# Half-height projection tiles, a parameter chain on GpSimd and an earlier set of rotation matrices in an attention-plus-SSM kernel

## The chip, the cores and the metric

The kernel runs on one core of one Trainium2 chip. The core has a matrix engine (TensorE, PE in the profile, with its weight loads as PEld), three engines for elementwise work (VectorE or DVE, ScalarE or ACT, GpSimd or POOL) and a synchronising engine (SyncE, SP), which here only issues transfers; ACT issues a few too. Each engine works through its own queue in order and waits on semaphores. The metric is device time in microseconds (us), lower is better; the profile's span is a little shorter than the time of the same execution.

## The reference

Two independent branches of 2048 tokens and 448 channels; their outputs stand side by side.

```python
# A: attention, 16 heads of 28, each token looks at 8 earlier tokens, 2 apart
qkv = x @ wqkv
logits = einsum("bhsd,bhswd->bhsw", q, kg) * scale      # kg: k at s, s-2, ..., s-14
attn = softmax(where(mask, logits, -1e9))
a = einsum("bhsw,bhswd->bhsd", attn, vg) -> [S, 448] @ wo
# B: a diagonal complex state-space layer with 448 states
Lam_bar = exp(exp(log_dt) * Lam)
B_bar = ((Lam_bar - 1) / Lam)[:, None] * Bmat
Bu = einsum("bld,pd->blp", x, B_bar)
h_t = Lam_bar * h_{t-1} + Bu_t
b = 2 * real(h @ Cmat^T) + x * Dskip
out = concatenate([a, b], -1)                            # bfloat16
```

## The kernel before

**Branch A.** Token p*16+j sits in partition p (0 to 127) with j = 0 to 15, so the eight keys of a token are in its own partition or, for the first few j, in a halo of 14 that transfers copy from the partition below. The x of branch A is transposed on PE, two j at a time (`g_xta`, group jp holds j = 2jp and 2jp+1; eight groups, taken from jp = 7 down), in four blocks of 112 channels, and DVE copies the result from PSUM to `xTA`. A projection (`proj(t, j)`, t = 0 for q, 1 for k, 2 for v) is then four matmuls of 112 contraction rows by 448 columns into one PSUM bank, which ACT copies out (L326) into `q_s`, `k_s` or `v_s`. There are 48 projections. `logits(hf, n, g)` puts DVE work on a list: for a half of the j (`hf`) and two offsets, one large product of q and k (L500) and a tree of additions (L503 to L517); eight of them. Softmax follows on DVE and ACT, then 40 products of weights and v (L573), which PE transposes and sums (L592) and multiplies by wo (L609).

**Branch B.** The states lie in seven groups of 64, real and imaginary parts in the two halves of the 128 partitions. Time is cut in pieces of T = 8 steps. Seven rotation matrices `R[k]` (one for each power of the state transition, built by DVE from small coefficients, L207), a pair `G` for B_bar (built the same way), and cosine and sine tables `tab` for the long scan all come from the parameters. These start as 28 short rows (`prow`, four small loads on ACT's queue), are transposed on PE (`params_in`), and go through a chain of about 35 tiny operations on [128, 7] and [128, 56] tiles: `params1` (to phases and exponents), `params_act` (exp and sines on ACT), `params2` (the rotation coefficients), `params3` (the coefficients of G). All of it but `params_act` is on DVE. `tables` (L299 to L302) computes the phases of the scan tables on DVE in three large operations, with R[1] to R[4] as scratch; six ACT operations turn them into `tab` (the list `acts`). `build_D` makes a diagonal matrix of Dskip on DVE, for the skip term.

PE work of branch B: `b_weights` (B times G), `b_x` (transposes of branch B's x, copied by ACT), `c_weights`, `ssm_in` (input sums and the 8 steps within a piece, first for four state groups, then for three), the scan over pieces (`scan_mul` and `scan_run` on DVE, `scan_pe` on PE), `ssm_mix` (adds the carried state to each step), `ssm_out` (eleven matmuls into one bank: C, then the skip diagonal; ACT copies it out).

**Order.** The schedule is written by hand. PE, ACT and SP get their instructions in program order; DVE work is put on a list with a cost (`add`) and taken off it when a running count of DVE time falls behind a running count of PE time (`pe`, `pump`, `fit`), or when `need` asks for it. The PSUM has eight banks, taken in turn by `bank()`: whoever asks for a bank waits until the tile that had it eight requests earlier has been read. Transfers take one of eight landing semaphores in turn; the ninth waits at its queue for the first to have landed. Before, ACT's queue starts with the four parameter rows, and SP's with x of branch A in five pieces of whole rows (tokens 14 and 15 first), the three thirds of wqkv, then B, branch B's x (rows cut in 384 and 64 columns) and C.

The main sequence is: groups 7 and 6, then k of j = 15 to 6 with the parameter chain between, q of j = 15 to 8 (after which the first logits can start), k of j = 5 to 0, all v with `b_weights`, q of j = 7 to 0 with `b_x`, then branch B's sums and scan, its outputs, and branch A's second half.

Of the kernel before, what the change touches and what calls it, by code (L numbers as in the profile page):

```python
# [14 lines left out]
J = 16  # L15
HALO = 14
# [20 lines left out]
def kernel(  # L37
# [48 lines left out]
    xnA = u1.rearrange("p (j d) -> p j d", j=J)  # L86
# [4 lines left out]
    wts = wbuf[0:KT].rearrange("p (a k n) -> p a k n", a=3, k=4)  # L91
# [3 lines left out]
    xTA = u3[0:KT].rearrange("p (k j n) -> p k j n", k=4, j=J)  # L95
# [3 lines left out]
    w_r = A_wqkv.rearrange("(k p) n -> p k n", p=KT)  # L99
    xB_r = B_x[0].rearrange("(c p j) d -> p c j d", p=128, j=T)  # L100

    def load_w(t):
        SP.dma_start(wts[:, t], w_r[:, :, t * D:(t + 1) * D])

    def load_x(lo, hi):
        SP.dma_start(xnA[:, lo:hi, :], xA_r[:, lo:hi, :])
# [5 lines left out]
    for i, vec in enumerate((B_Lambda_re, B_Lambda_im, B_log_dt, B_Dskip)):  # L112
        ACT.dma_start(prow[NT * i:NT * (i + 1)], vec.rearrange("(t i) -> t i", i=HS).unsqueeze(1).to_broadcast((NT, 2, HS)))
# [4 lines left out]
    load_x(4, 8)  # L118
    load_w(0)
    load_x(0, 4)  # L120
    load_w(2)
    SP.dma_start(Bn[0:HS, :, 0:D], half_rows(B_B_re))
# [73 lines left out]
    def tt(o, a_, b_, op):  # L196
        V.tensor_tensor(o, a_, b_, op)
        return o
# [23 lines left out]
    def params_in():  # L222
        tp = bank(BF16)
        PE.transpose(tp[:, 0:4 * NT], prow.rearrange("p a i -> p (a i)"), ident[0:4 * NT, 0:4 * NT])
        V.tensor_copy(prm.rearrange("p a b -> p (a b)"), tp[:, 0:4 * NT])
        ACT.activation(dt[:], ld, ACTF.Exp)
        dve(0.3)

    def params1():
        tt(are[:], dt[:], lre, ALU.mult)  # L230
        tt(th[:], dt[:], lim, ALU.mult)
        tt(rk[:], by_k(are), kkb, ALU.mult)
        V.tensor_scalar(f1[:], th[:], 1.0 / (2 * PI), None, ALU.mult)
        V.tensor_scalar(fT[:], th[:], float(T) / (2 * PI), None, ALU.mult)
        tt(yk[:], by_k(f1), kkb, ALU.mult)
        V.tensor_scalar(tk[:], yk[:], 1.0, MAGIC, ALU.mult, ALU.add)
        V.scalar_tensor_tensor(tk[:], tk[:], -MAGIC, yk[:], ALU.add, ALU.subtract)
        tt(den[:], lre, lre, ALU.mult)
        tt(t0[:], lim, lim, ALU.mult)
        tt(den[:], den[:], t0[:], ALU.add)  # L240
        V.reciprocal(den[:], den[:])
        dve(1.7)
# [7 lines left out]
    def params2():  # L250
        def two(ap):
            return ap.unsqueeze(3).to_broadcast((HS, T - 1, NT, 2))
        tt(sn[:], sn[:], rk[:], ALU.mult)
        V.tensor_copy(coef[0:HS, :, :, 1], two(sn[0:HS, 0:T - 1]))
        V.tensor_scalar(coef[HS:128, :, :, 0], two(sn[HS:128, 0:T - 1]), -1.0, None, ALU.mult)
        tt(cs[:], cs[:], rk[:], ALU.mult)
        V.tensor_copy(coef[0:HS, :, :, 0], two(cs[0:HS, 0:T - 1]))
        V.tensor_copy(coef[HS:128, :, :, 1], two(cs[HS:128, 0:T - 1]))

    def params3():  # L260
        a1, b1 = cs[:, 0], sn[:, 0]
        V.tensor_scalar(nr[:], a1, -1.0, None, ALU.add)
        tt(gre[:], nr[:], lre, ALU.mult)
        tt(t0[:], b1, lim, ALU.mult)
        tt(gre[:], gre[:], t0[:], ALU.add)
        tt(gre[:], gre[:], den[:], ALU.mult)
        tt(gim[:], b1, lre, ALU.mult)
        tt(t0[:], nr[:], lim, ALU.mult)
        tt(gim[:], gim[:], t0[:], ALU.subtract)
        tt(gim[:], gim[:], den[:], ALU.mult)  # L270
        V.tensor_copy(cg[0:HS, :, 0], gre[0:HS])
        V.tensor_copy(cg[0:HS, :, 1], gim[0:HS])
        V.tensor_scalar(cg[HS:128, :, 0], gim[HS:128], -1.0, None, ALU.mult)
        V.tensor_copy(cg[HS:128, :, 1], gre[HS:128])
        cg2 = cg.unsqueeze(3).to_broadcast((128, NT, 2, 2))
        V.tensor_copy(cgb[:, 0], cg2)
        tt(cgb[:, 1], cg2, cgb[:, 0], ALU.subtract)
# [10 lines left out]
    def build_D():  # L288
        V.tensor_copy(dsk[0:HS], prm[0:HS, 3, 0:NT:2])
        V.tensor_copy(dsk[HS:128, 0:3], prm[HS:128, 3, 1:NT:2])  # L290
        V.tensor_copy(dsk[HS:128, 3:4], prm[HS:128, 3, NT - 1:NT])
        V.tensor_tensor(dgD.rearrange("p (k n) -> p k n", k=4), ident.unsqueeze(1).to_broadcast((128, 4, 128)),
                        dsk.unsqueeze(2).to_broadcast((128, 4, 128)), ALU.mult)

    yy = tab.rearrange("p a t c -> p (a t c)").bitcast(F32).rearrange("p (t c) -> p t c", t=NT)
    tm = R[:, 1:5].rearrange("p k t n -> p (k t n)").bitcast(F32).rearrange("p (t c) -> p t c", t=NT)

    def tables():
        V.tensor_tensor(yy, iot.unsqueeze(1).to_broadcast((128, NT, NC)),  # L299
                        fT.unsqueeze(2).to_broadcast((128, NT, NC)), ALU.mult)  # L300
        V.tensor_scalar(tm, yy, 1.0, MAGIC, ALU.mult, ALU.add)
        V.scalar_tensor_tensor(tm, tm, -MAGIC, yy, ALU.add, ALU.subtract)  # L302
        for t in (slice(0, 4), slice(4, NT)):
            acts.append(lambda t=t: ACT.activation(tab[:, 1, t], tm[:, t], ACTF.Sin, scale=-2 * PI * SHR))
            acts.append(lambda t=t: ACT.activation(tm[:, t], tm[:, t], ACTF.Abs))
            acts.append(lambda t=t: ACT.activation(tab[:, 0, t], tm[:, t], ACTF.Sin, bias=hpib[:], scale=-2 * PI * SHR))


    def g_xta(jp):
        tp = bank(BF16)  # L310
        tpv = tp[0:KT].rearrange("p (k j n) -> p k j n", k=4, j=2)
        for kt in range(4):
            for jj in range(2):
                PE.transpose(tpv[:, kt, jj, :], xnA[:, 2 * jp + jj, KT * kt:KT * (kt + 1)], ident[:])  # L314
        V.tensor_copy(xTA[:, :, 2 * jp:2 * jp + 2, :], tpv)  # L315
        dve(0.65)
        load[0] += 0.45

    def proj(t, j):
        ps = bank()  # L320
        for kt in range(4):
            PE.matmul(ps[:, 0:D], xTA[:, kt, j, :], wts[:, t, kt, :], start=(kt == 0), stop=(kt == 3))  # L322
        src = ps[:, 0:D].rearrange("p (h d) -> p d h", h=H)
        dst = (q_s[:, :, j * H:(j + 1) * H] if t == 0 else
               k_s[:, :, HALO + j, :] if t == 1 else v_s[:, HALO + j])
        ACT.copy(dst, src)  # L326
        count[2] += 1
        if acts and count[2] > 18 and count[2] % 2 == 0:
            acts.pop(0)()
        pe(0.76)  # L330
# [137 lines left out]
    def ssm_out(j, cb):  # L468
        cols = slice(cb * 128, (cb + 1) * 128)
        ps = bank()  # L470
        for t in range(NT):
# [5 lines left out]
        PE.matmul(ps[:, 384:448], xT[:, jp, 6, cols], dgD[:, 384 + HS * jj:384 + HS * (jj + 1)], start=False, stop=True)  # L477
# [3 lines left out]
        pe(1.53)  # L481
# [3 lines left out]
    Ls = [Lf[:, 0:1024].rearrange("p (w n) -> p w n", w=W), Lf[:, 1024:2048].rearrange("p (w n) -> p w n", w=W)]  # L485
    m4 = Lf[:, 2048:2560].rearrange("p (w n) -> p w n", w=4)
    attn = u3[:, 5120:7168].rearrange("p (w n) -> p w n", w=W)
# [135 lines left out]

    g_xta(7)
    g_xta(6)
    proj(1, 15)
    proj(1, 14)
    params_in()
    g_xta(5)
    params1()  # L630
    proj(1, 13)
    proj(1, 12)
    params_act()
    g_xta(4)
    proj(1, 11)
    proj(1, 10)
    g_xta(3)
    add(1.2, params2)
    has_R = [add(0.6, lambda: build_R(0))]
    add(2.3, params3)  # L640
    has_G = add(1.1, build_G)
    proj(1, 9)
    proj(1, 8)
    g_xta(2)
    proj(1, 7)
    proj(1, 6)
    has_tab = add(5.2, tables)
    has_D = add(1.1, build_D)
    has_B2 = add(0.3, double_B)
    proj(0, 15)  # L650
    g_xta(1)
    proj(0, 14)
    g_xta(0)
    for j in range(13, 7, -1):
        proj(0, j)
    logits(1, 0, 3)
    for j in range(5, -1, -1):
        proj(1, j)
# [5 lines left out]
    for j in range(15, -1, -1):  # L664
        proj(2, j)
        if j % 2 == 0 and j > 0:
            b_weights(j // 2 - 1)
        elif j in (7, 3):
            b_x(0, j // 4)
    for k in range(1, T - 1):  # L670
        has_R.append(add(0.55, lambda k=k: build_R(k)))
    halo(lambda lo, hi, a_, b_: v_s[lo:hi, a_:b_])
    for j in range(7, -1, -1):
        proj(0, j)
        if j % 2 == 1:
            b_x(2 - j // 4, j // 2 % 2)
    for n_, g in enumerate((0, 1, 2, 3)):
        logits(0, n_, g)
# [8 lines left out]
    for n_ in range(8):  # L687
        next(first)
        if n_ in (1, 2):
            b_x(3, n_ - 1)  # L690
# [3 lines left out]
    need(has_tab)  # L694
    while acts:
        acts.pop(0)()
# [23 lines left out]
    ssm_mix(0, 2)  # L720
    banks = scan_pe(1, 1)
# [3 lines left out]
    need(has_D, *has_R)  # L725
    ssm_mix(0, 3)
    ssm_mix(0, 4)
    ssm_mix(0, 5)
    banks = scan_pe(1, 0)
# [11 lines left out]
    for cb in range(2):  # L741
        ssm_out(T - 1, cb)
    for j in range(T - 1):
        if j + 1 < T - 1:
            ssm_mix(1, j + 1)
        for cb in range(2):
            ssm_out(j, cb)
# [42 lines left out]
```

## Time and profile before

| | us |
|---|---|
| median of 3 runs (lowest, highest) | 166.61 (166.44, 167.23) |
| the profiled execution, its time | 167.04 |
| the profiled execution, its span | 165.2 |
| PE busy, DVE busy, ACT busy, POOL busy | 157.0, 146.2, 101.2, 2.9 |
| granted PE clock | full in all 40 slices |
| first transposes of x (PE) | 4.82 |
| second group of transposes, after a wait for its x | 6.56 |
| first product of the logits (DVE, L500) | 27.32 |
| first scan product (DVE, L427) | 74.73 |
| first product of weights and v (DVE, L573) | 119.62 |

Busy time on PE is the union of pipelined matmuls and does not say that each ran at its best rate; the pitch of matmuls in a row does. "[0.94 <-DVE wbuf L427]" behind a row of the timeline is idle time of that engine before the row, and what ended it. "x12" is a number of merged instructions. In the chain of waits a row is a start, a length and what held the end of the kernel in that time.

### The profile page before, as it was taken

How to read it: one execution, taken by the hardware profiler on the slowest of the kernel's cores; microseconds unless marked ns; L12 is line 12 of the kernel's file. 1: busy time of each engine (PE TensorE's matmuls, PEld its weight loads, DVE VectorE, ACT ScalarE, POOL GpSimd, SP SyncE). 2: the span in 40 equal slices, each digit the busy share in tenths (PEclk: the TensorE clock that was granted, in tenths of full speed). 3: DMA queues.
4: the chain of work that ended last, by engine and by line, in shares of the span. 5: the costliest groups of instructions: out<-in, count | busy, mean ns of one | idle time of the engine just before them, and what ended most of it. 6: DMA issues, size and time to landing. Idle time of an engine off the chain costs nothing.

```text
span 165.2 us, 3640 instructions
## 1 busy us (share of the span) xinstructions
PE 157.0 (95%) x1511; PEld 110.9 (67%) x1513; DVE 146.2 (89%) x178; ACT 101.2 (61%) x194; POOL 2.9 (2%) x23
## 2 busy tenths in 40 slices
PE   6799999999999999997997999999999999999992
PEld 6566655666667878774764666665659988877870
DVE  1377999999999999998999999999999999999911
ACT  3068568999997474693569865579431343436531
POOL 3000000000000000000010000000000000000000
PEclk9999999999999999999999999999999999999999
DMA  5999996796299000000000002111214001112112
GB/s 157 341 250 186 237 269 137 147 158 90 50 194 145 4 4 0 0 4 0 0 4 0 0 5 81 57 56 63 76 62 125 31 28 60 57 43 74 64 51 83
DMA packets 17164, 14.01 MB, mean 85 GB/s; under 512 B 6636, under 2 KB 16636, under 8 KB 17020
## 3 DMA queue, kind: packets, MB, share of 16 engines
q1 hardware_dynamic: 17063, 13.77, 35.5%
q8 instruction: 12, 0.20, 0.5%
q14 instruction: 5, 0.04, 0.1%
q10 hardware_dynamic: 84, 0.01, 0.0%
HBM read 6.89 MB, written 3.67 MB: 64 GB/s over the span
## 4 chain that ended last, share of the span: by engine, by line
PE 56%; DVE 33%; issue 6%; DMA 3%; SPq 0%; DVEq 0%
PE b L322 22%; DVE k_s L573 11%; PE b L472 7%; PE b L592 6%; DVE u L500 5%; PE b L609 5%; PE b L382 3%; DMA u<-in_A_x_dram 3%; DVE u L503 2%; PE b L314 2%; PE b L462 2%; PE b L460 2%; DVE k_s L577 2%; DVE R L207 2%; PE b L337 2%
## 5 line engine op out<-in xcount | busy, mean ns | idle before, releaser
L322 PE MATMUL b<-wbuf,u 112*128 112x448 bf16 x192 | 39.6, 352 | 0.0
L573 DVE TENSOR_TENSOR k_s<-u,v_s 128x1792 bf16<-128x1792 bf16 (+1 forms) x40 | 33.1, 897 | 0.0
L500 DVE TENSOR_TENSOR u<-q_s,k_s 128x7168 bf16<-128x7168 bf16 x8 | 31.1, 3887 | 0.2
L592 PEld LDWEIGHTS <-k_s 128*112 128x112 bf16 x448 | 26.9, 130 | 2.5 <-DVE k_s L577 0.7
L592 PE MATMUL b<-ident,k_s 128*112 128x128 bf16 x448 | 27.4, 219 | 0.3 <-DVE k_s L577 0.3
L322 PEld LDWEIGHTS <-u 112*128 112x128 bf16 x192 | 17.9, 98 | 14.0
L472 PE MATMUL b<-Cw,u 128*128 128x448 bf16 x112 | 23.8, 352 | 0.0
L402 ACT CAST u<-b 128x512 bf16<-128x512 f32 (+1 forms) x32 | 15.6, 542 | 11.2 <-PE b L401 8.8
L382 PE MATMUL b<-xT,BT 128*128 128x256 bf16 x168 | 20.7, 273 | 0.0
L382 PEld LDWEIGHTS <-BT 128*128 128x128 bf16 x168 | 16.2, 98 | 2.4 <-issue 0.2
L503 DVE TENSOR_TENSOR u<-u 128x3584 bf16<-128x3584 bf16 x8 | 16.2, 2023 | 0.2
L614 ACT CAST ya<-b 128x448 bf16<-128x448 f32 x15 | 8.1, 537 | 13.3 <-PE b L609 11.2
L479 ACT CAST yo<-b 128x448 bf16<-128x448 f32 x16 | 8.4, 528 | 11.6 <-PE b L477 8.2
L472 PEld LDWEIGHTS <-u 128*128 128x128 bf16 x112 | 10.3, 98 | 7.5
L609 PE MATMUL b<-u,q_s 112*128 112x448 bf16 x64 | 14.4, 352 | 0.0
L463 ACT CAST u<-b 128x512 bf16<-128x512 f32 (+1 forms) x28 | 13.3, 567 | 0.9 <-PE b L462 0.9
L602 ACT CAST q_s<-b 112x512 bf16<-112x512 f32 x15 | 7.8, 595 | 8.1 <-PE b L592 8.0
L326 ACT CAST k_s<-b 128x448 bf16<-128x448 f32 x16 | 8.0, 533 | 6.7 <-PE b L322 6.7
L326 ACT CAST q_s<-b 128x448 bf16<-128x448 f32 x16 | 8.6, 537 | 3.1 <-PE b L322 2.7
L460 PE MATMUL b<-u,ident 128*128 128x512 bf16 (+1 forms) x28 | 9.9, 352 | 0.0
L315 DVE COPY u<-b 112x1024 bf16<-112x1024 bf16 x8 | 5.4, 681 | 4.8 <-PE b L314 4.8
L462 PE MATMUL b<-u,R 128*128 128x255 bf16 x49 | 9.5, 273 | 0.0
(128 smaller groups left out, 199.0 us busy)
## 6 DMA issues: line engine op xcount, KB each, us to landing
out_dram<-yo SPq DMA_DIRECT2D x16, 112.0 KB, 1.7
out_dram<-ya SPq DMA_DIRECT2D x16, 112.0 KB, 1.7
u<-in_B_x_dram SPq DMA_DIRECT2D x2, 768.0 KB, 14.2
u<-in_A_x_dram SPq DMA_DIRECT2D x3, 448.0 KB
wbuf<-in_A_wqkv_dram SPq DMA_DIRECT2D x3, 392.0 KB, 7.9
k_s<-k_s SPq DMA_DIRECT2D x1, 784.0 KB
v_s<-v_s SPq DMA_DIRECT2D x1, 784.0 KB
k_s<-k_s SPq DMA_DIRECT2D x1, 588.0 KB
```

Source lines behind the costliest of these rows:

```text
L322: PE.matmul(ps[:, 0:D], xTA[:, kt, j, :], wts[:, t, kt, :], start=(kt == 0), stop=(kt == 3))
L326: ACT.copy(dst, src)
L382: PE.matmul(ps[:, i * NC:(i + 1) * NC], BT[:, t, kt, :], xT[:, jp, 2 * kt + jj, :], start=(kt == 0 and i == 0), stop=False)
L402: ACT.copy(Z[:, pr_[0]:pr_[0] + n, j, :], ps[:, 0:n * NC].rearrange("p (t c) -> p t c", t=n))
L460: PE.matmul(ps[:, 0:n * NC], ident[:], Z[:, sl, j, :], start=True, stop=False)
L463: ACT.copy(Z[:, sl, j, :], ps[:, 0:n * NC].rearrange("p (t c) -> p t c", t=n))
L472: PE.matmul(ps[:, 0:D], Z[:, t, j, cols], Cw[:, t, :], start=(t == 0), stop=False)
L500: V.tensor_tensor(pr[:], qv, kv, ALU.mult)
L503: V.tensor_tensor(pr[:, :, 0:14, :], pr[:, :, 0:14, :], pr[:, :, 14:28, :], ALU.add)
L573: V.tensor_tensor(pv_of(i), attn[:, s, H * j0:H * (j0 + nj)].rearrange("p (j h) -> p j h", h=H) .unsqueeze(2).to_broadcast((128, nj, DH, H ...
L592: PE.matmul(acc[kt // kb][0:KT, o:o + 128], pvf[:, jj, KT * kt:KT * (kt + 1)], ident[:], start=(s == 0 and o == 0), stop=(s == W - 1 and o ...
L609: PE.matmul(ps[:, 0:D], oTs[n_ % 3][:, kt, jj, :], wo_p[:, kt, :], start=(kt == 0), stop=(kt == 3))
```

## The change

- *Projections.* The 448 contraction rows are three tiles of 128 and one of 64. Of a pair of tokens, the even one has its last 64 channels in partitions 0 to 63 and the odd one in 64 to 127; one transpose turns both (`g_xta` has 7 transposes, before 8). `proj(t, hi, n)` now takes n tokens (four, or two): three full matmuls for each, into n banks, then the n half-height matmuls in a row, then n copies by ACT. Other PE work (`between`) stands between the tokens' full matmuls.
- *Loads.* x of branch A is loaded as 384 columns (SP) and 64 columns (ACT: tokens 8 to 15 first on its queue, tokens 0 to 7 after the parameter rows). The last 64 rows of wqkv are loaded twice, into both partition halves (for k on ACT's queue, for q and v on SP's).
- *Parameter chain.* The elementwise operations of `params1`, `params2`, `params3` go to POOL; one fused operation becomes two; the reciprocal stays on DVE, behind the tables. The parameter copy out of PSUM goes to ACT.
- *Skip diagonal.* Its three small copies go to POOL, the scaling to four ACT operations.
- *Order on DVE.* The tables come after the sixth transpose copy, in two parts with scratch in the tiles of v and C; then the reciprocal and R[0] to R[4] (mixed with the last two transpose copies); then the first logit product, the doubling of B and G. R[5] and R[6] come after the first product group of the other half. Before, R[0], G and the tables were ahead of the first product, and R[1] to R[6] came after four.
- *Order on PE and ACT.* Two pairs of `b_x` move from the last q projections into the sums of branch B, and so do the last three table operations of ACT. `ssm_out` is split in `out_open` (four state groups and the skip term) and `out_close`; the two openings of the last step go into the scan of the second half.

```diff
-    wts = wbuf[0:KT].rearrange("p (a k n) -> p a k n", a=3, k=4)
+    wts = wbuf.rearrange("p (a k n) -> p a k n", a=3, k=4)
...
+    def load_we(eng, t):
+        for a in range(2):
+            eng.dma_start(wts[HS * a:HS * (a + 1), t, 3], A_wqkv[384:448, t * D:(t + 1) * D])
...
-        SP.dma_start(xnA[:, lo:hi, :], xA_r[:, lo:hi, :])
+        SP.dma_start(xnA[:, lo:hi, :], xA_r[:, lo:hi, 0:384])
+    def load_xe(lo, hi):
+        ACT.dma_start(xeA[:, lo:hi, :], xA_r[:, lo:hi, 384:448])
...
+    load_xe(8, 16)
+    load_we(ACT, 1)
     load_x(14, 16)
     load_w(1)
     load_x(12, 14)
     load_x(8, 12)
     load_x(4, 8)
+    for i, vec in enumerate((B_Lambda_re, B_Lambda_im, B_log_dt, B_Dskip)):
+        ACT.dma_start(prow[NT * i:NT * (i + 1)], ...)
+    load_xe(0, 8)
     load_w(0)
+    load_we(SP, 0)
     load_x(0, 4)
     load_w(2)
+    load_we(SP, 2)
...
     def tt(o, a_, b_, op):
-        V.tensor_tensor(o, a_, b_, op)
+        POOL.tensor_tensor(o, a_, b_, op)
...
+        for k in range(4):
+            ACT.activation(dgD[:, 128 * k:128 * (k + 1)], ident[:], ACTF.Copy, scale=dsk[:, k:k + 1])
...
+    def proj(t, hi, n, *between, odd=False):
+        todo_ = list(between)
+        js = range(hi, hi - n, -1)
+        pss = {}
+        for j in js:
+            pss[j] = ps = bank()
+            for kt in range(3):
+                PE.matmul(ps[:, 0:D], xTA[:, j // 2, 2 * kt + j % 2, :], wts[:, t, kt, :], start=(kt == 0), stop=False)
+            pe(0.56)
+            if (odd or j % 2 == 0) and todo_ and j > js[-1]:
+                todo_.pop(0)()
+        for j in js:
+            rows = slice(HS * (j % 2), HS * (j % 2 + 1))
+            PE.matmul(pss[j][:, 0:D], xTA[rows, j // 2, 6, :], wts[rows, t, 3, :], start=False, stop=True)
+        for j in js:
+            ...
+            ACT.copy(dst, src)
...
+    g_xta(7)
+    proj(1, 15, 4, X(6), X(5), both(params_in, params1, X(4)), odd=True)
+    proj(1, 11, 4, X(3), X(2))
+    has_tab = add(5.3, tables)
+    params_act()
+    proj(1, 7, 2)
+    params2()
+    add(0.2, params3)
+    proj(0, 15, 4)
+    has_R = [add(0.6, lambda k=k: build_R(k)) for k in range(5)]
+    proj(0, 11, 4, X(1), X(0))
     logits(1, 0, 3)
+    has_B2, has_G = (0.3, double_B, None), (1.1, build_G, None)
+    todo[-2:-2] = [has_B2, has_G]
+    proj(1, 5, 2, act)
+    proj(1, 3, 4, act)
```

## The prediction

> **What bounds the kernel now.** First the engine totals: TensorE (PE) and VectorE (DVE) are both nearly full, so a saving on one alone may buy nothing.
>
> ```profile
> PE 157.0 (95%) x1511; PEld 110.9 (67%) x1513; DVE 146.2 (89%) x178; ACT 101.2 (61%) x194; POOL 2.9 (2%) x23
> DVE  1377999999999999998999999999999999999911
> DMA  5999996796299000000000002111214001112112
> ```
>
> The last two lines are 40 slices of 4.13 us: DVE is partly idle only in the first four, and the loads fill the first six. Next, stretches cut where DVE's work changes: stretch, length, busy PE (instructions), weight loads, DVE, ACT, POOL, clock, DMA share, GB/s.
>
> ```profile
> 27.32:60.60 33.28, 33.28 (x292) 22.46 (x291) 32.52 (x19) 28.71 (x52) 0.00 (x0) 1.00 0.56 100
> 60.60:74.70 14.10, 13.93 (x170) 10.62 (x167) 14.00 (x11) 10.28 (x19) 0.32 (x3) 1.00 0.00 1
> 119.60:145.20 25.60, 25.35 (x349) 21.10 (x346) 25.50 (x27) 8.99 (x18) 0.00 (x0) 1.00 0.19 59
> ```
>
> From the first logit product (27.32) on, DVE has hardly a gap. Then the timeline, for who waits for whom:
>
> ```profile
> 20.97 2.01 DVE L299 TENSOR_TENSOR tab<-iot,fT 128x1792 f32<-128x1792 f32 x1
> ...
> 23.83 0.53 ACT L326 CAST q_s<-b 128x448 bf16<-128x448 f32 x1 [0.23 <-PE b L322]
> ...
> 27.32 3.88 DVE L500 TENSOR_TENSOR u<-q_s,k_s 128x7168 bf16<-128x7168 bf16 x1
> ...
> 60.61 3.29 DVE L207 TENSOR_TENSOR R<-dup,coef 128x896 bf16<-128x896 bf16 x6
> ...
> 75.47 0.39 PE L437 MATMUL b<-wbuf,ident 128*128 128x512 bf16 x1 [0.94 <-DVE wbuf L427]
> ...
> 145.17 1.10 PE L592 MATMUL b<-ident,k_s 128*112 128x128 bf16 x16 [0.25 <-DVE k_s L577]
> ```
>
> The q columns of the first product are ready at 24.4 (the copy at 23.83), but DVE gets to it only at 27.32, behind the tables. PE waits for DVE at the scan (75.47) and once more at 145.17, after which it runs to the end. So the end is 145.17 plus 20.0 us of tail, and 145.17 hangs on when DVE starts the first product. I call that start L (27.32). PE must only keep up.
>
> **The change, part by part.** *PE.* The chain of waits has these pieces (start, length, what):
>
> ```profile
> 15.32 2.27 PE b L322 x12
> ...
> 57.42 1.31 PE b L382 x12
> 58.73 0.54 PE b L392 x8
> ```
>
> A full 448-column matmul is 2.27/12 = 0.19 us. Half-height matmuls on alternating rows (L392) take 0.135 a pair of 256 columns, a full one (L382) 0.109: a pair costs 1.24 full ones. Four tokens become 12 x 0.19 + 2 x 0.235 = 2.75 us, before 3.03. Twelve such groups save 3.4 us (bounds 0, no overlap, to 4.5, perfect overlap); 64 transposes become 56, 8 x 0.056 = 0.45. Sum 3.9 us of PE, worth time only if DVE lets it.
>
> *DVE.* It loses the parameter copy (0.2), the first chain (10.08 to 11.88, less the reciprocal, 1.6), the second (14.01 to 15.4, 1.4), the third (15.96 to 18.25, 2.3) and the diagonal (26.08 to 27.2, 1.0): 6.5 us, all ahead of L. Behind L, four rotation builds go out (4 x 0.55 = 2.2), while the G build (1.08) and the doubling of B (0.28) come in behind the first product: 0.83 less. So the span changes by (L - 27.32) - 0.83.
>
> *Where L lands.* Call X5 the start of the third transpose group (tokens 10, 11). From it PE runs: 0.39, three matmuls 0.57, parameters and next group 0.51, 0.57, first half pair 0.24; the first bank's copy (0.53) must end before the fifth token can have its bank, so 2.9. Then 4 x 0.57 + 2 x 0.39 + 0.47 = 3.5 and DVE's copy 0.6: 7.0. Then DVE alone: tables 2.01 + 1.09 + 2.03 and 0.1 for the split, reciprocal 0.2, five rotation builds 2.75, two transpose copies 1.2: L = X5 + 16.4. The q copies are done at X5 + 15.6, hidden behind this; without it they decide, 0.8 earlier.
>
> *X5.* Packet prices are estimates: the third slice moved 250 GB/s of mostly 896-byte rows, 57 ns each on 16 engines; the halo (448 bytes) moved 158 in slice nine, 45 ns; a line through both gives 54 ns at 768 bytes, 37 at 128. Before, x of tokens 12 and 13 was issued at 1.64 and landed at 6.52 (chain), with 2.9 us of packets up to its end: 2.0 us beside them. Now the rows of x are cut to 768 bytes and the last 64 columns come as 1024 packets of 128 bytes on ACT's queue. Up to tokens 8 to 11: (1024 x 54 + 512 x 57 + 1024 x 37)/16 = 7.6 us, so 0.74 + 2.0 + 7.6 = 10.4. The 128-byte load itself, first on its queue, has 2.4 us of packets: 5.1 if alone, 8.6 if every packet alternates with SP's; I take an equal share of time, 7.5, and X5 is 2.8 later, 10.3. They agree: X5 = 10.4 (bounds 8.4 and 11.5), L = 26.8.
>
> Each load in the changed instruction order waits for the landing of an earlier one, eight semaphores in turn. On ACT's queue the second parameter vector waits for the 128-byte load; behind it stand two more vectors, the second 128-byte load, and then ACT's table load and every copy. At 0.3 to 0.4 us an issue (four took 0.74 to 2.39 before) that second load goes out at 8.7 and lands between 13.0 and 16.6; its user needs it at X5 + 4.0 = 14.4. I take no wait (nearest is the solo transfer, since SP's queue is itself held by such waits); bound 2.2. On SP's queue the B loads now wait for it, 8 us later than before; what they feed starts after 30, and the k halo behind them needs to land by L + 18 (bound 1 us).
>
> *POOL.* No row shows POOL arithmetic. Bounds per operation: DVE's own chain, 1.8/12 = 0.15, and POOL's 128x128 select, 0.29. The first chain (13) ends by X5 + 6 and is awaited at X5 + 7. The next six start when ScalarE has its sines (X5 + 10.4) and end at 11.3 to 12.1; the first build wants them at 12.4. The last fifteen end by 16.6; the G build wants them at L + 4.2 = X5 + 20.6. All hidden, by 0.3 us at least; I take 0.25.
>
> [...]
>
> *ACT.* It takes four 128x128 scalings (0.25 to 0.53 each, by its 128x56 and 128x448 rows) and gives three table activations (0.89 + 0.92 + 1.04) to the stage after; it has 4.6 us free in 27.32 to 60.6. Two transpose copies (0.91 each) now stand ahead of the first state copy: PE then waits some 0.9, which the 0.94 at 75.47 absorbs; with that gone it would cost 0.9. The two early output sums fill PE's scan wait at 90: nothing, since DVE decides.
>
> *Sum.* Span 165.2 + (26.8 - 27.32) - 0.83 = 163.85. The profiled run took 167.04, 1.84 outside its span; the median is 166.61, so 166.6 - 1.35 = 165.3 us.
>
> **The rivals.** *All of PE's gain arrives* (0.10): 3.9 us off, 162.7. For it: PE is 95% busy; against: DVE's gapless stretches. *The start gives it back* (0.18): X5 at 11.4 or X3 a microsecond late, L = 27.8, 166.3, no change. *POOL is late* (0.20, slower): if each POOL operation costs about a rotation build (0.6), the six end at X5 + 14.0, so L is 1.6 later, and the fifteen end at X5 + 23.0, 0.8 after G wants them: 2.4 more, 167.7. It decides from 0.33 us an operation. Against: the POOL rows above. *The handshakes are late* (0.10, slower): the second 128-byte load lands at 8.6 + 1.2 + 2.0 + 5.9 = 17.7, L is 12.4 after it, 30.1: 168.6.
>
> **How the numbers follow.** My forecast, faster by about 0.8%, has 0.42, its own range 164.5 to 165.8. A measurement of this kernel tells about 0.5% (0.8 us) from no change. Faster 0.42 + 0.10 = 0.52, same 0.18, slower 0.30. The range, 163.4 to 168.2, reaches past the start's and POOL's cases and leaves out the full PE gain and the late handshakes, 0.20 together.
>
> **What would show it.** L500 starts at 26 to 27.5, with R built five times just before; PE's projections drop to 0.69 a token; PE waits at the scan again; POOL's 34 operations take 5 to 10 us and DVE waits for none of them. Wrong would be: L after 28; DVE idle before L207 with POOL named; X5 after 11.5; or DVE idle long anywhere past L, since then PE was the bound.

## The result, and the profile after

Four executions of the changed kernel took 164.56 to 164.90 us, median 164.66; four of the kernel before 166.44 to 167.23, median 166.68: a ratio of 0.9877, 95% interval 0.985 to 0.9904. The profiled execution has a span of 162.8 us, before 165.2. Twelve later executions (below, as an experiment) fell into two groups, six at 164.70 to 165.07 and six at 166.76 to 167.06, with a ratio of 0.9958 (0.9919 to 0.9997). Ratios leave out executions more than 1.5% above the fastest of the same kernel; only the kernel before had any, two to four in each later comparison (169.0 to 171.1 us). So the gain is 2 us or nothing, and which of the two is decided in the first 11 us. The profile here is of the first group.

Page of the changed kernel: engine totals, and the slices of VectorE and GpSimd.

```profile
PE 155.0 (95%) x1503; PEld 105.8 (65%) x1505; DVE 140.3 (86%) x143; ACT 101.6 (62%) x199; POOL 20.6 (13%) x59
...
DVE  1336989799999999998998999999999999999911
...
POOL 3050789910000000000010000000000000000000
```

TensorE lost 2.0 us of work, not the 3.9 of the forecast. VectorE lost 5.9, but its sixth and eighth slices (4.07 us each) have holes, and just there GpSimd is over 80% busy: it gained 17.7 us with 36 operations (33 of the chain, 3 of the skip diagonal), where the forecast counted 34 and put them at 5 to 10 us.

Its timeline (start, length, engine, line and operation; in brackets the idle time before it and who ended it):

```profile
7.67 0.50 PE L327 MATMUL b<-ident,u 128*128 128x128 bf16 x6
...
14.78 2.02 DVE L313 TENSOR_TENSOR tab<-iot,fT 128x1792 f32<-128x1792 f32 x1
...
17.17 0.52 POOL L211 TENSOR_TENSOR sn<-sn,rk 128x56 f32<-128x56 f32 x1 [4.51 <-ACT sn L258]
...
20.85 0.27 POOL L270 CAST coef<-cs 64x98 bf16<-64x98 f32 x1
...
21.15 1.16 DVE L221 TENSOR_TENSOR R<-dup,coef 128x896 bf16<-128x896 bf16 x2 [0.72 <-POOL coef L270]
...
24.91 3.88 DVE L535 TENSOR_TENSOR u<-q_s,k_s 128x7168 bf16<-128x7168 bf16 x1
24.99 3.85 POOL L284 COPY cg<-gre 64x7 f32<-64x7 f32 x1
...
28.78 0.22 POOL L285 COPY cg<-gim 64x7 f32<-64x7 f32 x1
...
30.19 1.09 DVE L221 TENSOR_TENSOR R<-dup,cgb 128x1792 bf16<-128x1792 bf16 x1 [1.20 <-POOL cgb L211]
...
31.43 0.61 PE L363 MATMUL b<-R,u 128*128 128x128 bf16 x8 [0.79 <-DVE R L221]
...
72.43 0.68 DVE L453 TENSOR_TENSOR wbuf<-u,tab 128x1024 bf16<-128x1024 bf16 x1
...
142.78 1.10 PE L627 MATMUL b<-ident,k_s 128*112 128x128 bf16 x16 [0.73 <-DVE k_s L612]
```

The reader is to see five things. The third transposes start at 7.67 (X5), the first logit product at 24.91 (L; before 27.32). VectorE waits for GpSimd twice, 0.72 and 1.20 us. A GpSimd copy of 64x7 values begins 0.08 us after the logit product and ends with it, after 3.85 us, while its twin behind it takes 0.22. The scan's first product comes at 72.43, before 74.73. And TensorE again waits for VectorE near the end, at 142.78 instead of 145.17, with the same 20.0 us behind it: the 2.4 us won by L are still there at the end.

### The profile page after: what moved, and what is told of

Read it like the earlier page. It is cut to its first block, busy times and chain, and to the rows that moved or that the text cites. A ratio compares the mean times of both kernels' runs of the same rounds, so it can differ in the third digit from the quotient of the medians.

```text
span 162.8 us, 3639 instructions
## 1 busy us (share of the span) xinstructions
PE 155.0 (95%) x1503; PEld 105.8 (65%) x1505; DVE 140.3 (86%) x143; ACT 101.6 (62%) x199; POOL 20.6 (13%) x59
## 3 DMA queue, kind: packets, MB, share of 16 engines
q1 hardware_dynamic: 18599, 13.56, 35.1%
q10 hardware_dynamic: 2324, 0.38, 1.3%
## 4 chain that ended last, share of the span: by engine, by line
DVE 64%; PE 18%; POOL 7%; issue 7%; ACT 2%; DVEq 0%; POOLq 0%
DVE u L535 17%; DVE k_s L608 11%; DVE u L538 10%; PE b L627 6%; DVE l L541 5%; PE b L644 5%; PE b L342 3%; DVE u L472 3%; DVE l L546 2%; POOL cg L284 2%; PE b L149 2%; DVE k_s L612 2%; DVE l L549 2%; DVE u L575 2%; DVE wbuf L453 1%
## 5 line engine op out<-in xcount | busy, mean ns | idle before, releaser
L342 PE MATMUL b<-wbuf,u 128*128 128x448 bf16 x144 | 31.1, 353 | 0.7 <-DVE u L330 0.7
L535 DVE TENSOR_TENSOR u<-q_s,k_s 128x7168 bf16<-128x7168 bf16 x8 | 31.1, 3887 | 0.2
L627 PE MATMUL b<-ident,k_s 128*112 128x128 bf16 x448 | 27.4, 219 | 0.9 <-DVE k_s L612 0.7
L342 PEld LDWEIGHTS <-u 128*128 128x128 bf16 x144 | 12.8, 98 | 11.7 <-issue 1.5
L500 PE MATMUL b<-Cw,u 128*128 128x448 bf16 x64 | 14.7, 353 | 0.0
L330 DVE COPY u<-b 128x896 bf16<-128x896 bf16 x8 | 5.0, 622 | 8.0 <-PE b L329 8.0
L512 PE MATMUL b<-Cw,u 128*128 128x448 bf16 x48 | 11.5, 353 | 0.0
L556 POOL MEMSET u<- 1x128 f32 (+3 forms) x10 | 1.3, 162 | 70.0 <-DVE u L552 70.0
L500 PEld LDWEIGHTS <-u 128*128 128x128 bf16 x64 | 6.3, 98 | 4.6
```

The source lines that it names most:

```text
L342: PE.matmul(ps[:, 0:D], xTA[:, j // 2, 2 * kt + j % 2, :], wts[:, t, kt, :], start=(kt == 0), stop=False)
L500: PE.matmul(ps[:, 0:D], Z[:, t, j, cols], Cw[:, t, :], start=(t == 0), stop=False)
L512: PE.matmul(ps[:, 0:D], Z[:, t, j, cols], Cw[:, t, :], start=False, stop=(t == NT - 1))
L535: V.tensor_tensor(pr[:], qv, kv, ALU.mult)
L627: PE.matmul(acc[kt // kb][0:KT, o:o + 128], pvf[:, jj, KT * kt:KT * (kt + 1)], ident[:], start=(s == 0 and o == 0), stop=(s == W - 1 and o ...
```

## The experiments

Times are medians; "first group" and "second group" are the two groups above.

**The parameter chain back on VectorE.** In `tt` and in `params1` to `params3`:

```diff
-        POOL.tensor_tensor(o, a_, b_, op)
+        V.tensor_tensor(o, a_, b_, op)
...
-        POOL.tensor_copy(cg[0:HS, :, 0], gre[0:HS])
+        V.tensor_copy(cg[0:HS, :, 0], gre[0:HS])
```

> The changed kernel with the parameter chain (L211 to L290) issued on VectorE again; all else as changed. Theory (VectorE decides the end, so the chain is worth its length there less the waits it caused on GpSimd): behind the tables VectorE gets about 3.7 us of small operations and loses its two waits for GpSimd (0.72 before the first rotation matrix, 1.20 before G): +1.8 us against the changed kernel's 164.7, so 166.4 us, and no VectorE wait for POOL ahead of L535. Rival (beside wide VectorE operations GpSimd's chain costs more than it takes off): 164.7 or less.

Measured: 166.75 us over 12 runs, six of them at 166.09 to 166.23, two at 168.3 and 168.4, four at 167.3 (their granted clock is 0.99, the others' 1.0); ratio 1.0019 (0.9986 to 1.0053) to the kernel before. The profiled execution, of the lowest times:

```profile
27.72 3.88 DVE L535 TENSOR_TENSOR u<-q_s,k_s 128x7168 bf16<-128x7168 bf16 x1
...
31.73 1.07 DVE L221 TENSOR_TENSOR R<-dup,cgb 128x1792 bf16<-128x1792 bf16 x1
...
73.95 0.68 DVE L453 TENSOR_TENSOR wbuf<-u,tab 128x1024 bf16<-128x1024 bf16 x1
```

The chain fills 20.31 to 23.98 without a gap and L is 2.8 us later than 24.91; G no longer waits, so that 1.5 us is left at the scan and at the end (span 164.3). The chain also stands ahead of two transpose copies there, for which TensorE waits 1.9 us. The move to GpSimd is worth 1.5 of the 2.4 us of span; the rival, that it costs more than it frees, is refuted.

**The kernel before with only that chain on GpSimd.** The same lines the other way round in the kernel before, the parameter copy on ScalarE, the order untouched.

> The kernel before with only the parameter chain on GpSimd; projections, loads, skip diagonal and the order of the rotation matrices as before. Theory (the move pays only together with the new order, which puts the tables ahead of the first rotation matrix): the first matrix, G and the tables are next in VectorE's queue while GpSimd still works, so VectorE stands for the chain and what it was relieved of comes back as waits: 166.5 to 168.0 us. Rival (the move off VectorE is itself the gain): 3 us of work less ahead of the first logit product, 164 to 165 us.

Measured: 168.14 us (six runs, 167.71 to 168.25), ratio 1.0088 (1.0063 to 1.0112): slower by 0.9%. Its waits (engine, what waited, for whom, total, times, longest):

```profile
DVE R L207 <- POOL cgb L197: 2.9, 1, 2.9
...
DVE R L207 <- POOL coef L259: 1.2, 1, 1.2
```

In the old order the first matrix and G stand ahead of the tables, so VectorE stands for 4.1 us in 13 to 20 us, with the tables, which need nothing of that, queued behind (and before that for 2.8 us, at the reciprocal, which here kept its place inside the chain). L falls at 27.97, later than 27.32. So the move loses in the old order and gains in the new one. That the tables alone make the difference was not tried apart: other parts of the order differ too, the reciprocal's place among them.

**Four of the five rotation matrices late again.**

```diff
-    has_R = [add(0.6, lambda k=k: build_R(k)) for k in range(5)]
+    has_R = [add(0.6, lambda k=k: build_R(k)) for k in range(1)]
...
-            for k in range(5, T - 1):
+            for k in range(1, T - 1):
```

> The changed kernel with one rotation matrix ahead of the first logit product and the other four after the first group of the other half, about where the kernel before had them. Theory (VectorE is idle in wait for the last q copy anyway, so matrices built there are free): L535 starts at 23.4 to 23.6 instead of 24.91, bounded by the last q copy; the four matrices, 2.4 us, come back in the gapless part; G still waits for GpSimd: +1.0 to +2.3 us at the scan, 165.5 to 166.9 us. Rival (the sum of VectorE's work is the same, so the place is worth nothing): 164.5 to 164.9 us.

Measured: 165.91 us over 12 runs, seven at 165.52 to 165.93, five at 167.0 to 167.8. The profiled execution is of the second group (span 166.0) and is read beside one of the changed kernel of that group (span 165.2), whose rows stand below it:

```profile
25.81 3.89 DVE L535 TENSOR_TENSOR u<-q_s,k_s 128x7168 bf16<-128x7168 bf16 x1 [0.56 <-ACT q_s L353]
...
68.62 3.30 DVE L221 TENSOR_TENSOR R<-dup,coef 128x896 bf16<-128x896 bf16 x6
...
75.63 0.69 DVE L453 TENSOR_TENSOR wbuf<-u,tab 128x1024 bf16<-128x1024 bf16 x1
```

```profile
27.26 3.88 DVE L535 TENSOR_TENSOR u<-q_s,k_s 128x7168 bf16<-128x7168 bf16 x1
...
74.80 0.68 DVE L453 TENSOR_TENSOR wbuf<-u,tab 128x1024 bf16<-128x1024 bf16 x1
```

L comes 1.45 earlier and now waits for the last q copy; the four matrices take 2.1 us back later (six in 3.30 us, in the changed kernel two in 1.15): +0.8 at the scan and in the span. The direction is the theory's, the size just under its range. Matrices built ahead of L were partly free.

**The changed kernel again.** No edit.

> The changed kernel itself, unaltered, on the chip and beside the runs of the other three. Two of the kernels above showed two groups of times some 2 us apart (163.4 and 165.5 us; 165.6 and 167.6 us), and in the profiles of the later group TensorE's first transposes take 0.85 us for six where the changed kernel's took 0.50, until about 10.5 us. Theory (a clock of TensorE that rises only in part of the executions by the end of the 34 warm-up products belongs to the common start, not to the edits): here too most executions lie at 164.5 to 164.9 us and some at 166.5 to 167 us. Rival (it came from the edits): all within 0.4 us of 164.66.

Measured: the two groups told of above. The profiled execution took 166.96 us; its TensorE:

```profile
4.96 0.85 PE L327 MATMUL b<-ident,u 128*128 128x128 bf16 x6
...
6.63 1.30 PE L342 MATMUL b<-wbuf,u 128*128 128x448 bf16 x3 [0.72 <-DVE u L330]
7.72 0.85 PE L327 MATMUL b<-ident,u 128*128 128x128 bf16 x6
...
9.59 0.85 PE L327 MATMUL b<-ident,u 128*128 128x128 bf16 x6
...
11.20 0.51 PE L327 MATMUL b<-ident,u 128*128 128x128 bf16 x6
```

and the same instructions in the profile of 162.8 us:

```profile
4.86 0.50 PE L327 MATMUL b<-ident,u 128*128 128x128 bf16 x6
...
6.13 0.74 PE L342 MATMUL b<-wbuf,u 128*128 128x448 bf16 x3 [0.72 <-DVE u L330]
6.71 0.50 PE L327 MATMUL b<-ident,u 128*128 128x128 bf16 x6
```

Six transposes take 0.85 against 0.50 us, three products 1.30 against 0.74. A merged length holds the end of its last product; from start to start three products take 1.09 us (6.63 to 7.72) against 0.58 (6.13 to 6.71). So in this profile TensorE runs at 0.53 of its rate, to about 10.5 us; the profile of the kernel with four matrices late, of the second group too, has the same 0.85 and 1.30. The granted clock does not show it (0.997 in both of the changed kernel); the starts do. X5 is 9.59 instead of 7.67, L 27.26 instead of 24.91, and the gain is gone. The theory holds: the groups belong to the start. Of 26 executions of the kernel before in this comparison 24 lie at 165.92 to 167.45 without a break, and two at 169.9 and 170.1 with a granted clock of 0.99. Beside the other experiments four of its 40 stand at 168.3 to 169.1 and one at 171.1 with a clock of 1.0, so that a rare second group of its own is not excluded. The low rate at least occurs there too, as the profile of the kernel before with the chain on GpSimd shows:

```profile
4.95 1.91 PE L315 MATMUL b<-ident,u 128*112 128x128 bf16 x16
6.80 1.69 PE L323 MATMUL b<-wbuf,u 112*128 112x448 bf16 x8
```

Sixteen transposes take 0.12 us each from 4.95 to 6.80, twice the 0.056 of full rate (eight in 0.45, 10.78 to 11.23 in the kernel before). But the profile shows no wait between them, and the eight products from 6.80 to 8.42 take 0.20 each, where eight from 11.23 to 12.75 in the kernel before take 0.19: the rate has risen.

**Filling TensorE's first wait.** In the second group the low rate lasts to about 10.5 us. In both profiles of the changed kernel TensorE waits 0.72 us behind the first transposes; here seven products stand in that place:

```diff
     g_xta(7)
+    for _ in range(7):
+        PE.matmul(warm[:, 0:128], ident[:], ident[:], start=True, stop=True)
     proj(1, 15, 4, X(6), X(5), both(params_in, params1, X(4)), odd=True)
```

> The changed kernel with seven more products on the identity right behind the first transposes, in the 0.72 us in which TensorE waits for the copy of its first transposed tokens. [...] Rival (the low rate is set by the chip's state at the start, whatever TensorE does there): two groups as before, some 2 us apart.

Measured: 165.03 us, six runs, 164.69 to 165.15, none in the second group; ratio 0.9882 (0.9846 to 0.9919). Its TensorE:

```profile
4.95 0.85 PE L327 MATMUL b<-ident,u 128*128 128x128 bf16 x6
...
5.70 0.67 PE L680 MATMUL b<-ident 128*128 128x128 bf16 x7
6.62 0.74 PE L342 MATMUL b<-wbuf,u 128*128 128x448 bf16 x3 [0.25 <-DVE u L330]
7.20 0.50 PE L327 MATMUL b<-ident,u 128*128 128x128 bf16 x6
```

This is the clearest of the runs: the beginning is that of the second group (0.85), yet by 6.62 three products take 0.74. With the wait filled the rate rises some 4 us sooner, and of 2.4 us of span about 0.5 is left (span 163.3 against 162.8). The filled wait is all that this kernel changes. Without filling, six of twelve executions fell into the second group, with it none of six, and none of the six of a later kernel that is so filled, whose profile also begins low (0.85).

So the rival's two groups did not come. Unfilled, the second group lies 2.1 us above the first, 1.3% of 165. How the wait acts on the rate no run shows. In the profile with the column ends on SP's queue (below) the first transposes are low as well (0.82), the same wait of 0.72 us follows, and yet three products take 0.74 us at 7.10.

**The sines a group of tokens earlier.**

```diff
-    proj(1, 11, 4, X(3), X(2))
+    proj(1, 11, 4, both(params_act, X(3)), X(2))
     has_tab = add(5.3, tables)
-    params_act()
```

> The changed kernel with the exponential and the sines of the parameter chain one group of tokens earlier on ScalarE (from about 12.1 us instead of 15.25, ahead of four k copies). Theory (VectorE waits 0.72 and 1.20 us because GpSimd's chain starts late and is then held up beside the tables): both waits go, L535 starts at 24.2 instead of 24.91 and the scan's first product (L453) up to 1.9 us earlier; TensorE, which waits only 0.21 us for VectorE at the scan and gains the 0.79 us that it now waits for G, becomes the limit there, so -0.8 to -1.2 us, 163.5 to 163.9 us. Rival (GpSimd's chain is too slow however early it starts): the waits stay, 164.7 us.

Measured: 164.46 us, three runs at 163.33 to 163.62 and three at 165.30 to 165.62: some 1.5 us below the changed kernel in either group, more than the 0.8 to 1.2 of the theory. Its interval, 0.9814 to 0.9926, mixes the two. With the first wait filled too:

> The last kernel with the sines early as well. Theory (both losses add: the waits for GpSimd's chain, 1.3 us, and the low rate at the start): one group at 163.3 to 164.2 us. Rival: two groups at 163.4 and 165.5 us as with the sines alone, or no gain over the last kernel.

Measured: 163.63 us, six runs, 163.27 to 164.01; ratio 0.9805 (0.9771 to 0.9839), which beats both kernels. Its VectorE:

```profile
20.83 1.11 DVE L221 TENSOR_TENSOR R<-dup,coef 128x896 bf16<-128x896 bf16 x2
...
24.56 3.88 DVE L535 TENSOR_TENSOR u<-q_s,k_s 128x7168 bf16<-128x7168 bf16 x1
...
29.12 1.09 DVE L221 TENSOR_TENSOR R<-dup,cgb 128x1792 bf16<-128x1792 bf16 x1 [0.48 <-POOL cgb L211]
...
71.36 0.68 DVE L453 TENSOR_TENSOR wbuf<-u,tab 128x1024 bf16<-128x1024 bf16 x1
```

The wait before the first matrix is gone, G's fell from 1.20 to 0.48, and the scan comes 1.56 us earlier than in the kernel with the filled wait alone (72.92). The theory had TensorE take over as the limit at -1.2; it no longer waits at the scan, but did not hold VectorE up by more than 0.1 us there (VectorE's own wait for it grew from 0.47 to 0.56). The 0.48 that is left is another copy beside L535 (L287, 3.69 us).

**GpSimd copies that nobody waits for.** Beside L535 a copy of 64x7 values lasted 3.85 us, its twin behind it 0.22. Here are 16 more copies:

```diff
+        for k in range(16):
+            POOL.tensor_copy(spare[:], dsk[0:HS])
         for k in range(4):
             ACT.activation(dgD[:, 128 * k:128 * (k + 1)], ident[:], ACTF.Copy, scale=dsk[:, k:k + 1])
```

> The changed kernel with 16 more GpSimd copies of 64x4 values behind the skip diagonal's three, of a tile that nobody waits for, so that they fall beside the logit products and their halvings. [...] Rival (the long copies are waits on semaphores that the profile adds to the operation): the 16 copies take 0.2 us each and end within 4 us.

Measured: 164.96 us over ten runs, eight of them at 164.73 to 165.08, two at 166.8. One line's operations (shortest, median and longest in ns, first and last start), and VectorE's timeline:

```profile
L307 POOL COPY spare<-dsk x16: 666/1066/3932, 33.8 to 60.5; 64x4 f32<-64x4 f32 x16
```

```profile
33.74 1.09 DVE L544 TENSOR_TENSOR l<-u 128x1792 bf16<-128x1792 bf16 x1
34.94 3.89 DVE L538 TENSOR_TENSOR u<-q_s,k_s 128x7168 bf16<-128x7168 bf16 x1
```

Between 33.7 and 61.1 VectorE ran 16 such products; 16 copies of 64x4 values took 27.4 us, one to each, the shortest (0.67) about as long as VectorE's shortest (0.69), the longest (3.93) as its longest (3.89). VectorE kept its lengths (3.88 to 3.89 and 2.02 to 2.03 us, in the changed kernel 3.88 to 3.89 and 2.02), and the time did not move. So the long copies are not waits on semaphores (for these the profile names none), and the length was a loss of GpSimd alone here. In the changed kernel it reached VectorE where that waited for GpSimd, 0.72 and 1.20 us. What makes the copies long no run shows.

**The skip diagonal on VectorE.** Three copies and one product, queued behind the first product group, in place of the three GpSimd copies and four scalings:

```diff
-        for k in range(4):
-            ACT.activation(dgD[:, 128 * k:128 * (k + 1)], ident[:], ACTF.Copy, scale=dsk[:, k:k + 1])
+        V.tensor_tensor(dgD.rearrange("p (k n) -> p k n", k=4), ident.unsqueeze(1).to_broadcast((128, 4, 128)),
+                        dsk.unsqueeze(2).to_broadcast((128, 4, 128)), ALU.mult)
```

> The changed kernel with the skip diagonal built on VectorE again (three copies and one 128x512 product, 1.04 us by their starts in the kernel before), in the gapless part ahead of the second group of logits; the three copies leave GpSimd and four scalings of 1.31 us together leave ScalarE. Theory (VectorE sets the scan): scan and end 0.9 to 1.1 us later, 165.5 to 165.8 us. Rival (TensorE sets it, or ScalarE's four scalings delayed the projections' evictions as much): 164.4 to 164.9 us.

Measured: 166.26 us over 12 runs, eleven at 165.90 to 166.32. TensorE's waits:

```profile
74.15 0.39 PE L463 MATMUL b<-wbuf,ident 128*128 128x512 bf16 x1 [0.80 <-DVE wbuf L453]
...
143.77 1.10 PE L627 MATMUL b<-ident,k_s 128*112 128x128 bf16 x16 [0.73 <-DVE k_s L612]
```

143.77 against 142.78: 0.99 us later. L was 0.13 later in this execution (25.04), so 0.86 of the 1.03 us that the work takes on VectorE (34.40 to 35.43) arrive; the rest falls into a gap of 0.2 us that VectorE otherwise has behind that product group. So time spent there behind L reaches the end nearly one for one. (The times lie some 0.4 us above the theory's range. VectorE's last copy is 0.98 later, 160.59 against 159.61, and the span 1.4: the 0.4 stands behind it, and why is open.)

**Half-height products unpaired.** The half-height product follows its token's three full ones:

```diff
             for kt in range(3):
                 PE.matmul(ps[:, 0:D], xTA[:, j // 2, 2 * kt + j % 2, :], wts[:, t, kt, :], start=(kt == 0), stop=False)
+            rows = slice(HS * (j % 2), HS * (j % 2 + 1))
+            PE.matmul(ps[:, 0:D], xTA[rows, j // 2, 6, :], wts[rows, t, 3, :], start=False, stop=True)
```

> The changed kernel with each half-height product right behind its token's three full ones, so that no two half-height products of different rows stand side by side; the same number of products. Theory (pairing is what makes four tokens cheaper than before, and TensorE, which waits only 0.21 us for VectorE at the scan, has no room left): 12 groups lose at least 0.28 us each (3.03 against 2.75), and 36 more changes between full and half height, beside which the profile shows weight loads idle for 0.37 us, may cost more: +3 to +12 us, 167.6 us or more. Rival (VectorE alone decides, TensorE has room): +0.5 to +1.5 us, 165.2 to 166.2 us.

Measured: 174.97 us (four runs), ratio 1.0539 (1.0485 to 1.0592). TensorE and the first scan product here, then TensorE in the changed kernel:

```profile
41.45 0.36 PE L344 MATMUL b<-wbuf,u 64*128 64x448 bf16 x1
41.75 0.74 PE L342 MATMUL b<-wbuf,u 128*128 128x448 bf16 x3
42.42 0.36 PE L344 MATMUL b<-wbuf,u 64*128 64x448 bf16 x1
...
84.18 0.69 DVE L452 TENSOR_TENSOR wbuf<-u,tab 128x1024 bf16<-128x1024 bf16 x1 [7.53 <-ACT u L427]
```

```profile
26.47 2.44 PE L342 MATMUL b<-wbuf,u 128*128 128x448 bf16 x12
28.84 0.55 PE L348 MATMUL b<-wbuf,u 64*128 64x448 bf16 x4
29.33 0.93 PE L342 MATMUL b<-wbuf,u 128*128 128x448 bf16 x4
```

A token takes 0.97 us alone (42.42 less 41.45) and 0.715 in fours (2.86 from 26.47 to 29.33, by four): 48 x 0.255 = 12.2 us of TensorE, of which about 10 reach the end (174.97 less 164.85, the middle of the first group). Here TensorE is the limit: VectorE stands 7.53 us at the scan, for copies of sums that come late. By subtraction TensorE has some 2 us of room below VectorE in the changed kernel, an estimate, about what the change saved it (2.0): VectorE decides, but not by much. Halves without their pair would have been dearer than four products of 112 rows (0.757 a token).

**The column ends on SP's queue.**

```diff
-        ACT.dma_start(xeA[:, lo:hi, :], xA_r[:, lo:hi, 384:448])
+        SP.dma_start(xeA[:, lo:hi, :], xA_r[:, lo:hi, 384:448])
...
-    load_we(ACT, 1)
+    load_we(SP, 1)
```

> The changed kernel with the 64-column ends of the tokens and of the k weights on SP's queue, ahead of or among the full-height loads, and no longer on ScalarE's. Theory (two queues side by side are what makes the small loads cost nothing: 0.50 us of issue for the ends and 1.2 us for the weight ends go ahead of the second token load on one queue, and 1024 packets of 128 bytes over 16 engines take 0.9 us at 14.6 ns each): the third transposes start 1 to 2.5 us later than 7.67, and L535 as much: 165.7 to 167.2 us. Rival (the loads have room): X5 at 7.7 and 164.5 to 164.9 us.

Measured: 165.71 us over nine runs, seven at 165.45 to 165.98; ratio 0.996 (0.993 to 0.999). TensorE at the start, and the changed kernel's queues (packets, MB, share of 16 engines' time; q10 is ScalarE's):

```profile
5.45 0.82 PE L327 MATMUL b<-ident,u 128*128 128x128 bf16 x6 [0.28 <-DMA u<-in_A_x_dram]
...
8.79 0.51 PE L327 MATMUL b<-ident,u 128*128 128x128 bf16 x6
```

```profile
q1 hardware_dynamic: 18599, 13.56, 35.1%
q10 hardware_dynamic: 2324, 0.38, 1.3%
```

X5 moves by 1.1 us, and 0.8 of it is seen in the times. Part of the 1.1 is the low rate of the first transposes (0.82), so that the loads alone account for some 0.6 (5.45 against 4.86). The second queue is worth under a microsecond, and its packets are cheap: 0.013 x 162.8 x 16 / 2324 = 14.6 ns each on average, 2048 of the 2324 being the ends of 128 bytes.

## Why the prediction was right, step by step

*VectorE decides, TensorE must only keep up*: right. From L to the scan it is 47.41 us before and 47.52 now, and VectorE's rows give the difference: by their starts four builds less are -2.14, G and the doubling +1.18, the wait for G +1.20, a smaller gap -0.11. From the scan to the last wait it is 70.44 and 70.35. So of TensorE's 2.0 us nothing arrives on its own, and the skip diagonal on VectorE moved the end by nearly its own length. "Everything of TensorE's gain arrives" is refuted.

*The span changes by (L - 27.32) - 0.83*: with L = 24.91 and G's wait, (24.91 - 27.32) - 0.83 + 1.20 = -2.04; measured -2.30 at the scan (by starts the 0.83 is 0.96, and the gap is 0.11 smaller), -2.39 at the last wait, -2.4 in the span.

*TensorE's saving, 3.9 us*: too high. A group of four took 2.86 us, not 2.75 (0.715 a token, not 0.69): six full products take 1.14 us ahead of transposes (10.39 to 11.53) but 1.23 ahead of half-height products (11.92 to 13.15), and the four halves 0.49 instead of 0.47. 12 x (3.03 - 2.86) = 2.0, and TensorE's busy time fell by 2.0 in all. It decided nothing: the sign "PE waits at the scan again" did not come, only 0.2 us of it is left.

*X5 = 10.4*: the worst-sized term. It was 7.67 at full rate and 9.59 at the low one, which the sum did not contain. The price of 37 ns for a 128-byte packet, off a line through two other sizes, was 14.6 by the mean of that queue; with it the same sum gives 9.0, so its other terms were too dear as well. The only wait for a load on TensorE ahead of L was 0.3 us (PEld, before transposes of x), and the queues of waiting issues delayed nothing that L needs.

*GpSimd hidden at 0.25 us an operation*: wrong, and the rival "POOL is late" had the price. One of the prediction's own signs of being wrong came true, VectorE idle before the rotation builds with GpSimd named. The six operations behind the sines took 3.95 us (17.17 to 21.12), 0.66 each; the forecast's rival put 0.6. They ended at X5 + 13.5 and the last fifteen at X5 + 22.5, near its 14.0 and 23.0. The waits were 0.72 and 1.20, together 1.9 us, where the rival reckoned 1.6 and 0.8, together 2.4: VectorE came to the first build at X5 + 12.8 instead of 12.4, and since its first wait was short it came to G sooner. The length went with what VectorE did beside: from 28.78 on, while VectorE made a copy of 0.28 us and then waited up to 30.19, six small GpSimd operations took 0.18 to 0.25 us each, and three copies 0.99, 1.99 and 3.85 beside VectorE products of 1.09, 2.02 and 3.88.

*L = X5 + 16.4*: 17.2, the 0.72 being the difference's greater part.

So the forecast of 165.3 lay 0.6 us above the measured 164.66 and 1.7 below the second group. It was right in its mechanism (VectorE, by way of L). Its sum was right in part by luck: a start 2.7 us too late in the reckoning stood against 1.9 us of waits for GpSimd left out. It was luck, too, that all four executions of the first measurement fell into the first group; six of the later twelve showed no gain. With the low rate, L = 27.26 is "the start gives it back" (L = 27.8, 166.3), by another cause: the low rate, not the loads.

What stays open: what share of executions falls into the second group (6 of 12 and 0 of 4 for the changed kernel; 3 of 6, 2 of 10, 1 of 12, 2 of 12, 1 of 4 and 3 to 5 of 12 for others with the same start), and why the same wait of 0.72 us goes with a low rate to 10.5 us in one execution and not in another.

## What to carry to other kernels

Small operations moved from VectorE to GpSimd are not hidden by being few: here GpSimd copies of 256 and 448 values lasted to the end of the VectorE product beside them (up to 3.93 us, against 0.18 to 0.22 while VectorE made a small copy or waited), so move them only where VectorE has other work queued ahead of the operation that needs them, and start them early. A warm-up at the front does not settle TensorE's rate: behind the same 34 products it was full in the profile of 162.8 us and 0.53 of that in the one of 165.2. Look at the spacing of the first products in more than one execution, and fill the first wait (six of twelve executions in the second group without, none of twelve with it). Half-height products paid in neighbours and in groups: by the starts one alone holds its place for 0.30 us, two in a row for 0.29 together (15.27 to 15.56 in the changed kernel), four for 0.49.

## What the runs showed of the hardware

- TensorE ran at 0.53 of its rate to about 10.5 us in one execution of the changed kernel (three products take 1.09 us from start to start, against 0.58 in another) while the granted clock reads 0.997 in both.
- A GpSimd copy of 256 values took 0.67 to 3.93 us beside VectorE products of 0.69 to 3.89; 16 of them took 27.4 us, and VectorE's products kept their 3.88 to 3.89 and 2.02 to 2.03 us. Begun while VectorE waited, such a copy took 0.18 (30.10 in the changed kernel).
- A change between 128 and 64 rows on TensorE cost time on both sides: an unpaired half-height product holds its place for 0.30 us (41.45 to 41.75), one of four in a row for 0.12 (28.84 to 29.33); three full products between unpaired halves hold theirs for 0.67 (41.75 to 42.42), three of twelve in a row for 0.59 (26.47 to 28.84). Beside it the profile shows 18.5 us of idle weight loads before the 48 unpaired halves.
- The packets of the second queue, mostly of 128 bytes, took 14.6 ns each on average, those of the first 49 ns (0.351 x 162.8 x 16 / 18599).
